# Top-32 attention and a two-layer MLP on one core: row blocks, interleaved VectorE steps, smaller MLP chunks, other weight loads

## The chip, the core and the metric

The kernel runs on one NeuronCore of a Trainium2 chip. The core has TensorE (PE in the profile, its weight loads PEld), VectorE (DVE), ScalarE (ACT), GpSimd (POOL) and SyncE (SP), which issues nearly all DMAs; each runs its own instructions in order. The metric is the device time of one execution in microseconds, median of several runs.

## The reference

For 8 batches, 8 heads, 576 positions and 64 dimensions in a head, each row of scores keeps its 32 largest values, and the rest is masked away before the softmax. The result, 4608 tokens of 512 values, goes through two matrices with a PReLU between them.

```python
scores = scale * np.matmul(q, k.transpose(0, 1, 3, 2))
kth = np.partition(scores, -top_k, axis=-1)[..., -top_k:-top_k + 1]
scores = np.where(scores >= kth, scores, -1000000000.0)
scores = scores - np.max(scores, axis=-1, keepdims=True)
attn = np.exp(scores)
attn = attn / (np.sum(attn, axis=-1, keepdims=True) + 1e-09)
attn_out = np.matmul(attn, v)
x = attn_out.transpose(0, 2, 1, 3).reshape(B * S, H * D)
h = x @ w_in                                  # 512 x 2048
g = np.maximum(h, 0.0) + alpha * np.minimum(h, 0.0)
out = g @ w_out                               # 2048 x 512
```

## The kernel before

Heads are taken in pairs (32 pairs, four for each batch). A *duo* is the work unit of the attention: 128 query rows of the two heads of a pair ("n", row block j = 0 to 3), or the last 64 rows of the four heads of two pairs ("m"). There are 18 duos in a batch and 144 in all. In batches 0 to 6 the duos go pair by pair: all four row blocks of pair e, those of pair e+1, then their "m". In the last batch they go by row block: block 0 of its four pairs, then block 1, and so on.

The main loop `for n in range(ND + 8)` is a software pipeline written out by hand. Every engine is wrapped in `Ordered`, so each runs exactly in the order of the program. One pass of the loop holds, for different duos:

- `st_phase2(n-2)` on VectorE: the largest 8 of y for both halves (`p<-y`), then eq, pk, and the threshold `KT`.
- `st_count(n-1)` on ScalarE: two sign passes `sg` with a count, biased by `p9`; `st_exit(n+1)`: the scores from PSUM to `s_sb`; `st_y(n-1)` on GpSimd: y = s times sg.
- `st_phase1(n)` on VectorE: twelve maxima over 96 values (`up` and `small`), bot, top, hi, neg, n8, and the ninth value of `p9`.
- `st_relu(n-2)` on ScalarE and `st_sub(n-2)` on GpSimd: pushes the values under the threshold down; `st_exp(n-3)`: the exponential into `w`, and a transposing DMA `wT<-w` on SP.
- `st_av(n-5)` on TensorE: attention times V into `xo` (or `xm`), where V's appended column of ones gives the sum; `st_norm(n-5)` on VectorE: `rz`, the reciprocal, and `x`.
- `st_qk(n+2)` on TensorE: the scores of a later duo into `ps_sc`.
- `prep(n, 4)`: transposes K and Q of a pair that begins within four duos on TensorE (`tps`, `tpt`); ScalarE copies K to `kT`, VectorE copies Q to `qT`. `loads(n, 7)` issues the loads of K, Q and V of a pair together, `casts(n)` turns V to bf16 on GpSimd.
- `f_unit()` and `o_unit()`: the MLP in small pieces. A unit of the first matmul is four matmuls into `ph` and a ReLU into `gT`, which alternates between VectorE and ScalarE (`relu`). A part of the second is five matmuls into `pz`; four parts make 128 tokens, and the last of them is followed by ScalarE's copy `o_sb` and the output DMA. Credits `fo` and `oo` (1.9 and 1.2 per pass) decide how many pieces are issued; towards the end the credits grow.

PReLU is split: relu(h) goes through w_out scaled by 1 - alpha (`w_out_b`), and the linear rest through one 512 x 512 matrix `w_lin_b` = w_in times alpha times w_out, which `weights()` computes in the first passes. It does so in units, two for each pass: load a piece of w_in and cast it on GpSimd; load a piece of w_out and scale it twice on ScalarE; transpose w_in by DMA; four `lin` units of 16 matmuls.

A batch's x reaches the MLP (`mlp_ready`) when all its pairs are transposed (`xT<-x`, one DMA for each pair). The MLP then takes the 576 tokens as one chunk, 32 units of 288 tokens; in the last batch it takes each row block by itself.

PSUM has eight banks: four for the scores (`ps_s`), one each for `small` (`ps_d`), for `ph` and the transposes together (`ps_h`), for `pz` (`ps_z`) and for `xo` (`ps_x`). All pools in PSUM have one buffer. In SBUF the staging pool `stg` has two buffers for each of K, Q and V, `qk_p` four, `gp` two. Behind `fast_path` stands `general_path`, which runs only where a flag says that the thresholds were not found; for these inputs it does not run.

Nearly all instructions are issued through `Ordered.call`, line 31, so that the profile's rows have that line, and the tiles' names tell them apart.

Of the kernel before, what the change touches and what calls it, by code (L numbers as in the profile page):

```python
# [17 lines left out]
NG = 6  # L18
# [17 lines left out]
def fast_path(tc, q, k, v, moe_w_in, moe_w_out, moe_alpha, out, flag):  # L36
# [17 lines left out]
    for b in range(B):  # L54
        p0 = KPB * b
        if b < B - 1:
            for e in (p0, p0 + 2):
                duos += [("n", p, j) for p in (e, e + 1) for j in range(4)]
                duos.append(("m", e, e + 1))
        else:  # L60
            duos += [("n", p, j) for j in range(4) for p in range(p0, p0 + 4)]
            duos += [("m", p0, p0 + 1), ("m", p0 + 2, p0 + 3)]
# [6 lines left out]
    with ExitStack() as ctx:  # L69
        pool = lambda name, bufs, **kw: ctx.enter_context(tc.tile_pool(name=name, bufs=bufs, **kw))  # L70
        const = pool("const", 1)
        stg = pool("stg", 2)
        io = pool("io", 4)
        qk_p = pool("qk", 4)
# [3 lines left out]
        gp = pool("gp", 2)  # L78
# [6 lines left out]

        ident_f = const.tile([128, 128], FP32, name="ident_f")
        make_identity(nc, ident_f)

        small = ps_d.tile([128, 512], FP32, name="small")
        io9 = small[:, 500:509]  # L90
        for i in range(9):
            DVE.memset(io9[:, i:i + 1], float(2 * i - 63 + S))
        KT = const.tile([128, ND, 2], FP32, name="KT")
        NV = 6
        v1s = [const.tile([128, 5, 2, 65], BF16, name=f"v1_{i}") for i in range(NV)]
        for t in v1s:
            POOL.memset(t, 1.0)
        ws = [const.tile([128, 2, 640], BF16, name=f"w_{i}") for i in range(3)]
        for t in ws:
            POOL.memset(t[:, :, S:640], 0.0)  # L100
        xs = [const.tile([128, 5, 128], BF16, name=f"x_{i}") for i in range(4)]
        for t in xs:
            POOL.memset(t[64:128, 4, :], 0.0)
        w_in_b = [const.tile([128, DFF], BF16, name=f"w_in_b{i}") for i in range(4)]
        w_out_b = [const.tile([128, DMODEL], BF16, name=f"w_out_b{i}") for i in range(NFT)]
        w_lin_b = [const.tile([128, DMODEL], BF16, name=f"w_lin_b{i}") for i in range(4)]
        alpha_sb = const.tile([128, NFT], FP32, name="alpha_sb")
        alpha1m = const.tile([128, NFT], FP32, name="alpha1m")
# [9 lines left out]
        def load_one(p, which, src):  # L118
            t = stg.tile([128, 5, 128], FP32, name=f"{which}_st", tag=f"{which}_st")
            for h in range(2):  # L120
                SP.dma_start(
                    t[:, 0:4, 64 * h:64 * h + 64],
                    src[2 * p + h, 0:512, :].rearrange("(c p) d -> p c d", p=128),
                )
                SP.dma_start(t[0:64, 4, 64 * h:64 * h + 64], src[2 * p + h, 512:S, :])
            st[which, p] = t

        def transpose_one(p, which, eng):
            t = st.pop((which, p))
            dst = qk_p.tile([128, S], FP32, name=f"{which}T", tag=f"{which}T")  # L130
            copy = ACT.copy if eng is ACT else DVE.tensor_copy
# [43 lines left out]
        def st_phase1(n):  # L175
            s = T["s", n]
            o = 240 * (n % 2)
            up = two.tile([128, 2, NG // 2, 8], FP32, name="up", tag="up")
            lo = small[:, o:o + 48].rearrange("p (i g c) -> p i g c", i=2, g=NG // 2)
            top = small[:, o + 48:o + 96].rearrange("p (i g c) -> p i g c", i=2, g=NG // 2)  # L180
            hi = small[:, o + 96:o + 112].rearrange("p (i c) -> p i c", i=2)
            n8 = small[:, o + 112:o + 128].rearrange("p (i c) -> p i c", i=2)
            for i in range(2):
                for g in range(NG):
                    DVE.max(out=(lo if g % 2 else up)[:, i, g // 2, :], in_=s[:, i, GW * g:GW * g + GW])


            bot = two.tile([128, 2, NG // 2, 8], FP32, name="bot", tag="bot")
            DVE.tensor_tensor(bot, up, lo[:, :, :, ::-1], ALU.min)
            DVE.tensor_tensor(top, up, lo[:, :, :, ::-1], ALU.max)  # L190
            neg = two.tile([128, 2, 32], FP32, name="neg", tag="neg")
            for i in range(2):
                DVE.max(out=hi[:, i, :], in_=bot[:, i, :, :])
            DVE.tensor_scalar(neg[:, :, 0:24].rearrange("p i (g c) -> p i g c", g=NG // 2), top, -1.0, None, ALU.mult)
            DVE.tensor_scalar(neg[:, :, 24:31], hi[:, :, 0:7], -1.0, None, ALU.mult)
            for i in range(2):
                DVE.max(out=n8[:, i, :], in_=neg[:, i, 0:31])
            p9 = three.tile([128, 2, 9], FP32, name="p9", tag="p9", bufs=4)
            DVE.tensor_scalar(p9[:, :, 0:1], n8[:, :, 7:8], -1.0, None, ALU.mult)
            T["p9", n] = p9  # L200
# [16 lines left out]

        def st_phase2(n):
            y, p9, cs = T.pop(("y", n)), T.pop(("p9", n)), T.pop(("cs", n))
            for i in range(2):  # L220
                DVE.max(out=p9[:, i, 1:9], in_=y[:, i, :])
            eq = small[:, 240 * (n % 2) + 128:240 * (n % 2) + 146].rearrange("p (i c) -> p i c", i=2)
            DVE.tensor_tensor(eq, io9.unsqueeze(1).to_broadcast([128, 2, 9]),
                              cs.unsqueeze(2).to_broadcast([128, 2, 9]), ALU.is_equal)
            pk = two.tile([128, 2, 9], FP32, name="pk", tag="pk")
            DVE.scalar_tensor_tensor(out=pk, in0=eq, scalar=BIG, in1=p9, op0=ALU.mult, op1=ALU.mult)
            DVE.tensor_reduce(out=KT[:, n, :].unsqueeze(2), in_=pk, op=ALU.add, axis=AX.X)

# [40 lines left out]

        xT = {}  # L270
        done = {}

        def st_norm(n):
            d = duos[n]
            xo = T.pop(("xo", n))
            m, w = (128, 2) if d[0] == "n" else (64, 4)
            rz = two.tile([128, 4], FP32, name="rz", tag="rz")
            DVE.reciprocal(rz[0:m, 0:w], xo[:, :, 64])
            if d[0] == "n":
                _, p, j = d  # L280
                DVE.tensor_tensor(xs[p % 4][:, j, :].rearrange("p (h d) -> p h d", h=2), xo[:, :, 0:64],
                                  rz[:, 0:2].unsqueeze(2).to_broadcast([128, 2, 64]), ALU.mult)
            else:
                for i in range(2):
                    DVE.tensor_tensor(xs[d[1 + i] % 4][0:64, 4, :].rearrange("p (h d) -> p h d", h=2),
                                      xo[:, 2 * i:2 * i + 2, 0:64],
                                      rz[0:64, 2 * i:2 * i + 2].unsqueeze(2).to_broadcast([64, 2, 64]),
                                      ALU.mult)

        def st_xT(n):  # L290

            d = duos[n]
            ps_ = d[1:2] if d[0] == "n" else d[1:]
            for p in ps_:
                b, kk = p // KPB, p % KPB
                j = d[2] if d[0] == "n" else 4
                if b < B - 1 and j < 4:
                    continue
                if ("xT", p) not in T:
                    T["xT", p] = xp.tile([128, 5, 128], BF16, name=f"xT{kk}", tag=f"xT{kk}")  # L300
                t = T["xT", p]
                if b < B - 1:
                    SP.dma_start_transpose(t, xs[p % 4].rearrange("p a b -> p (a b)"))
                else:
                    SP.dma_start_transpose(t[:, j:j + 1, :], xs[p % 4][:, j, :])
                done[b, j] = done.get((b, j), 0) + 1
                if done[b, j] == KPB:
                    mlp_ready(b, j)
# [5 lines left out]
        def mlp_ready(b, j):  # L314
            xt = [T["xT", KPB * b + kk] for kk in range(KPB)]
            flat = [t.rearrange("p a b -> p (a b)") for t in xt]
            if b < B - 1:
                tok0, ntok = 0, S
            else:
                tok0, ntok = 128 * j, (128 if j < 4 else 64)  # L320
# [3 lines left out]
            big = ntok == S  # L324
            cw = 288 if big else 4 * ntok

            def unit(i):
                if i == 0:

                    while oq and oq[0][0] <= me - 2:  # L330
                        oq.pop(0)[1]()
                    hold["g"] = gp.tile([128, NFT, ntok], BF16, name="gT", tag="gT" if big else "gs")
                gt = hold["g"]
                ph = ps_h.tile([128, cw], FP32, name="ph", tag="h")
                if big:
                    f, t0 = i // 2, 288 * (i % 2)
                    for kk in range(4):
# [472 lines left out]
```

## Time and profile before

| | |
|---|---|
| runs | 1291.47, 1293.12, 1298.55 us; median 1293.12 |
| profiled execution | 1296.23 us, span 1294.2 us |
| mean granted TensorE clock | 0.797 |
| busy: TensorE, VectorE, ScalarE, GpSimd | 881.2, 896.7, 836.6, 759.8 us |
| chain that ended last | DVE 46%, PE 24%, ACT 13%, DMA 6%, issue 4%, SPq 3%, POOL 3% |
| starts of `s_sb<-ps_sc` for duos 0, 18, 36, 54, 72, 90, 108, 126 | 11.3, 183.5, 335.1, 469.4, 602.6, 738.6, 875.3, 1040.2 us |

No engine is busy for more than 69% of the span. A row of the profile has the start or the busy time, then engine, operation, output and inputs. Where a row names a releaser in brackets, the engine sat idle for that long before it, until the releaser was done. "Granted clock" is the share of full speed that TensorE was given.

### The profile page before, as it was taken

How to read it: one execution, taken by the hardware profiler on the slowest of the kernel's cores; microseconds unless marked ns; L12 is line 12 of the kernel's file. 1: busy time of each engine (PE TensorE's matmuls, PEld its weight loads, DVE VectorE, ACT ScalarE, POOL GpSimd, SP SyncE). 2: the span in 40 equal slices, each digit the busy share in tenths (PEclk: the TensorE clock that was granted, in tenths of full speed). 3: DMA queues.
4: the chain of work that ended last, by engine and by line, in shares of the span. 5: the costliest groups of instructions: out<-in, count | busy, mean ns of one | idle time of the engine just before them, and what ended most of it. 6: DMA issues, size and time to landing. Idle time of an engine off the chain costs nothing.

```text
span 1294.2 us, 18779 instructions
## 1 busy us (share of the span) xinstructions
PE 881.2 (68%) x5282; PEld 481.4 (37%) x5282; DVE 896.7 (69%) x4247; ACT 836.6 (65%) x1416; POOL 759.8 (59%) x675
## 2 busy tenths in 40 slices
PE   5542436677777867777787787687776387778655
PEld 3221213334334433443344344444343143444433
DVE  4873444788878988788878886888788276762620
ACT  3756554777777777787867775777577265663530
POOL 4873433667766777676757775777577265442530
PEclk9955567576788988998888877997788668989767
DMA  4544541426252534443433533343424413221220
GB/s 107 123 118 96 111 99 38 89 44 109 53 114 62 99 72 97 83 90 80 90 74 87 89 82 77 82 96 69 105 54 99 91 31 69 51 46 45 57 53 20
DMA packets 346000, 102.00 MB, mean 79 GB/s; under 512 B 337168, under 2 KB 337184, under 8 KB 345888
## 3 DMA queue, kind: packets, MB, share of 16 engines
q1 hardware_dynamic: 345888, 100.73, 37.5%
q8 instruction: 44, 0.72, 0.2%
q14 instruction: 68, 0.56, 0.1%
HBM read 36.71 MB, written 9.44 MB: 36 GB/s over the span
## 4 chain that ended last, share of the span: by engine, by line
DVE 46%; PE 24%; ACT 13%; DMA 6%; issue 4%; SPq 3%; POOL 3%; ACTq 0%; POOLq 0%
DVE small L31 15%; DVE p L31 11%; DVE up L31 6%; PE pz L31 6%; PE ph L31 6%; PE ps_sc L31 4%; PE tps L31 4%; SPq L31 3%; ACT sg L31 3%; DVE gT L31 3%; DMA w_st<-in_moe_w_out_dram 2%; ACT r L31 2%; DVE neg L31 2%; ACT s_sb L31 2%; DVE x L31 2%
## 5 line engine op out<-in xcount | busy, mean ns | idle before, releaser
L31 POOL TENSOR_TENSOR y<-s_sb,sg 128x576 f32<-128x576 f32 x288 | 361.8, 1277 | 409.6 <-ACT sg L31 409.6
L31 POOL TENSOR_TENSOR s_sb<-s_sb,r 128x576 f32<-128x576 f32 x288 | 361.7, 1278 | 61.9 <-ACT r L31 61.9
L31 PE MATMUL ps_sc<-kT,qT 64*128 64x64 f32 (+3 forms) x1280 | 256.3, 533 | 102.4 <-ACT s_sb L31 102.3
L31 PE MATMUL ph<-xT,w_in_b 128*128 128x288 bf16 (+2 forms) x1216 | 212.7, 316 | 162.6 <-DVE gT L31 63.2
L31 ACT ACTIVATE sg<-s_sb,p 128x576 bf16<-128x576 f32 x288 | 220.4, 767 | 66.6 <-DVE p L31 65.4
L31 DVE MAX8 p<-y 128x8 f32<-128x576 f32 x288 | 204.2, 747 | 44.2 <-POOL y L31 44.2
L31 ACT ACTIVATE r<-s_sb,KT 128x576 bf16<-128x576 f32 x288 | 207.2, 768 | 33.7 <-DVE KT L31 27.5
L31 PEld LDWEIGHTS ps_sc<-kT,qT 64*128 64x128 f32 (+1 forms) x1280 | 126.1, 216 | 268.9 <-issue 148.2
L31 DVE MAX8 small<-s_sb 128x8 f32<-128x96 f32 x864 | 216.7, 251 | 0.0
L31 DVE MAX8 up<-s_sb 128x8 f32<-128x96 f32 x864 | 211.1, 244 | 3.1 <-ACT s_sb L31 3.1
L31 PEld LDWEIGHTS <-w_in_b 128*128 128x128 bf16 x1216 | 114.8, 111 | 201.8 <-issue 164.9
L31 PE MATMUL pz<-w_out_b,gT 128*128 128x512 bf16 (+1 forms) x640 | 187.0, 420 | 0.0
L31 ACT ACTIVATE w<-s_sb 128x1152 bf16<-128x1152 f32 x144 | 165.6, 1150 | 1.1 <-POOL s_sb L31 1.1
L31 ACT COPY s_sb<-ps_sc 128x1152 f32<-128x1152 f32 x144 | 158.2, 1098 | 7.0 <-PE ps_sc L31 7.0
L31 PEld LDWEIGHTS <-wT 128*128 128x128 bf16 (+3 forms) x1600 | 106.1, 108 | 119.7 <-issue 42.9
L31 PE MATMUL xo<-v,wT 128*128 128x65 bf16 (+1 forms) x1280 | 113.1, 212 | 49.0 <-DMA wT<-w 28.2
L31 DVE TENSOR_SCALAR gT<-ph 128x288 bf16<-128x288 f32 (+2 forms) x122 | 56.7, 465 | 110.9 <-PE ph L31 110.8
L31 ACT ACTIVATE gT<-ph 128x288 bf16<-128x288 f32 (+2 forms) x122 | 50.8, 416 | 120.3 <-PE ph L31 120.3
L31 DVE COPY qT<-tps 128x512 f32<-128x512 f32 x32 | 22.1, 691 | 117.2 <-PE tps L31 117.2
L31 PEld LDWEIGHTS <-gT 128*128 128x128 bf16 (+1 forms) x640 | 71.0, 111 | 79.8 <-issue 30.8
L31 PE MATMUL pz<-w_lin_b,xT 128*128 128x512 bf16 (+1 forms) x160 | 70.6, 441 | 2.8 <-ACT o_sb L31 2.7
L31 ACT COPY kT<-tps 128x512 f32<-128x512 f32 x32 | 18.7, 584 | 74.4 <-PE tps L31 74.4
(54 smaller groups left out, 733.3 us busy)
## 6 DMA issues: line engine op xcount, KB each, us to landing
k_st<-in_k_dram SPq DMA_DIRECT2D x64, 128.0 KB, 2.5
q_st<-in_q_dram SPq DMA_DIRECT2D x64, 128.0 KB, 2.5
v_st<-in_v_dram SPq DMA_DIRECT2D x64, 128.0 KB, 2.4
out_dram<-o_sb SPq DMA_DIRECT2D x32, 256.0 KB, 2.5
w_st<-in_moe_w_in_dram SPq DMA_DIRECT2D x16, 256.0 KB, 3.7
w_st<-in_moe_w_out_dram SPq DMA_DIRECT2D x16, 256.0 KB, 3.0
wT<-w SPq DMA_TRANSPOSE x144, 3.4
k_st<-in_k_dram SPq DMA_DIRECT2D x64, 16.0 KB, 2.2
```

What stands on the lines that cost most here:

```text
L31: return self.tc.keep_in_program_order(f(*a, **kw))
```

## The change

The duos of all batches now go by row block. VectorE's steps of a pass stand in one function, `dve_slot`, where steps of duos n, n-1, n-2 and n-5 alternate, with the two `f_unit()` calls between them (`norm_a` issues `rz`, `norm_b` issues `x`); `st_av` comes first in the pass. Every ReLU is on VectorE. Outside the prologue both copies of a prep are on ScalarE. The MLP takes a batch in two chunks, 256 tokens (row blocks 0 and 1) and 320 tokens (blocks 2 to 4), with one unit for each of the 16 blocks of d_ff. x is kept by row block and transposed by one DMA for a block of four pairs. w_in comes by four casting DMAs of GpSimd's queue; w_out's loads (`w_load`) are issued apart from their use (`w_use`), and GpSimd does one of the two scalings. V is loaded apart from K and Q. Three preps stand ahead of the loop. Buffers: `stg` 3, `qk` 6, `gp` 3, `io` 2, a new `wst` 5, V tiles 8.

```diff
-        if b < B - 1:
-            for e in (p0, p0 + 2):
-                duos += [("n", p, j) for p in (e, e + 1) for j in range(4)]
-                duos.append(("m", e, e + 1))
...
+        duos += [("n", p, j) for j in range(4) for p in range(p0, p0 + KPB)]
+        duos += [("m", p0, p0 + 1), ("m", p0 + 2, p0 + 3)]
...
-        stg = pool("stg", 2)
-        io = pool("io", 4)
-        qk_p = pool("qk", 4)
+        stg = pool("stg", 3)
+        io = pool("io", 2)
+        wst = pool("wst", 5)
+        qk_p = pool("qk", 6)
...
-        gp = pool("gp", 2)
+        gp = pool("gp", 3)
...
+        def dve_slot(n):
...
+                for i in range(2):
+                    for g in range(NG):
+                        DVE.max(out=(lo if g % 2 else up)[:, i, g // 2, :],
+                                in_=s[:, i, GW * g:GW * g + GW])
+                        if i == 0 and g == 1 and on(n - 2):
+                            DVE.tensor_reduce(out=KT[:, n - 2, :].unsqueeze(2), in_=T.pop(("pk", n - 2)),
+                                              op=ALU.add, axis=AX.X)
+                bot = two.tile([128, 2, NG // 2, 8], FP32, name="bot", tag="bot")
+                DVE.tensor_tensor(bot, up, lo[:, :, :, ::-1], ALU.min)
+                DVE.tensor_tensor(top, up, lo[:, :, :, ::-1], ALU.max)
...
+            if on(n - 5):
+                norm_a(n - 5)
+            if on(n):
+                neg = two.tile([128, 2, 32], FP32, name="neg", tag="neg")
+                for i in range(2):
+                    DVE.max(out=hi[:, i, :], in_=bot[:, i, :, :])
+                DVE.tensor_scalar(neg[:, :, 0:24].rearrange("p i (g c) -> p i g c", g=NG // 2), top,
+                                  -1.0, None, ALU.mult)
+            if on(n - 5):
+                norm_b(n - 5)
+            if on(n - 1):
...
+                DVE.tensor_tensor(eq, io9.unsqueeze(1).to_broadcast([128, 2, 9]),
+                                  cs.unsqueeze(2).to_broadcast([128, 2, 9]), ALU.is_equal)
+                DVE.max(out=p9[:, 0, 1:9], in_=y[:, 0, :])
+            if on(n):
+                DVE.tensor_scalar(neg[:, :, 24:31], hi[:, :, 0:7], -1.0, None, ALU.mult)
+            f_unit()
+            if on(n):
+                for i in range(2):
+                    DVE.max(out=n8[:, i, :], in_=neg[:, i, 0:31])
+            if on(n - 1):
+                DVE.max(out=p9[:, 1, 1:9], in_=y[:, 1, :])
+            if on(n):
...
+                DVE.tensor_scalar(p9n[:, :, 0:1], n8[:, :, 7:8], -1.0, None, ALU.mult)
+            f_unit()
+            if on(n - 1):
...
+                DVE.scalar_tensor_tensor(out=pk, in0=eq, scalar=BIG, in1=p9, op0=ALU.mult, op1=ALU.mult)
...
+        def chunk_of(b, j):
+            if b < B - 1:
+                return (b, 0, 2) if j < 2 else (b, 2, 5)
+            return (b, j, j + 1)
...
+            SP.dma_start_transpose(xT[c][:, :, o:o + m], xs.pop((b, j))[0:m, :])
...
-                    while oq and oq[0][0] <= me - 2:
+                    while oq and oq[0][0] <= me - 3:
...
-                    relu(gt[:, f, t0:t0 + 288], ph)
+                DVE.tensor_scalar(gt[:, e_n * i:e_n * i + e_n, :].rearrange("p a t -> p (a t)"), ph,
+                                  0.0, None, ALU.max)
...
-                ACT.activation(w_out_b[f], s, AF.Copy, scale=alpha1m[:, f:f + 1])
-                ACT.activation(hold["wl"][:, f, :], s, AF.Copy, scale=alpha_sb[:, f:f + 1])
+                ACT.activation(w_out_b[f], s, AF.Copy, scale=alpha1m[:, f:f + 1])
+                POOL.tensor_scalar(hold["wl", f // 8][:, f % 8, :], s, alpha_sb[:, f:f + 1], None, ALU.mult)
...
+                if ("v", p) not in loaded and first[p] <= n + ahead - 4:
+                    loaded.add(("v", p))
                     load_one(p, "v", vv)
...
-                    transpose_one(p, "k", ACT)
-                    transpose_one(p, "q", DVE)
+                    transpose_one(p, "k", ACT.copy)
+                    transpose_one(p, "q", DVE.tensor_copy if n < 0 else ACT.copy)
...
-                if p not in cast and p in loaded and first[p] <= n + 3:
+                if p not in cast and first[p] <= n - 2:
...
+        for kk in range(4):
+            POOL.dma_start(w_in_b[kk], moe_w_in[128 * kk:128 * kk + 128, :])
         for n in range(ND + 8):
-            loads(n, 7)
+            loads(n, 6)
...
-            end = n >= ND - 14
-            fo = min(fo + (4.5 if end else 1.9), 6.0)
-            oo = min(oo + (2.5 if end else 1.2), 4.0)
+            end = n >= ND - 12
+            fo = min(fo + (4.5 if end else 1.9), 5.0)
+            oo = min(oo + (2.6 if end else 1.25), 4.0)
+            if on(n - 5):
+                st_av(n - 5)
             if on(n - 1):
                 st_count(n - 1)
             if on(n + 1):
                 st_exit(n + 1)
             if on(n - 1):
                 st_y(n - 1)
+            dve_slot(n)
...
             casts(n)
             o_unit()
             if on(n + 2):
                 st_qk(n + 2)
             o_unit()
             if on(n - 5):
                 st_xT(n - 5)
-            prep(n, 4)
+            prep(n, 3)
+            for _ in range(2):
+                if n >= 1 and w_load:
+                    w_load.pop(0)()
+                if n >= 3 and w_use:
+                    w_use.pop(0)()
```

While `w_use` still holds units, neither `f_unit` nor `o_unit` issues anything.

## The prediction

> **What bounds the kernel now.** I read the chain that ended last (46% VectorE, 24% TensorE) and then divided the span by its loop passes. One pass of the main loop is called a slot here; it issues the steps of duos n+2 to n-5. The scores' copies `s_sb<-ps_sc` (one for each slot) start at 11.3 us (first), 216 us (duo 20), 335.1, 469.4, 602.6, 738.6, 875.3 us (every 18th from duo 36), 1040.2 (duo 126) and 1211 us (the last). So there are a stage in which the weights are made (205 us), batches of 133 to 137 us, the last batch, and 83 us behind the last copy. An undisturbed slot on VectorE, from the timeline:
> ```profile
> 701.80 1.41 DVE L31 MAX8 p<-y 128x8 f32<-128x576 f32 x2
> 703.13 0.16 DVE L31 TENSOR_TENSOR small<-small,cs 128x18 f32<-128x18 f32 x1
> 703.63 0.25 DVE L31 MAX8 up<-s_sb 128x8 f32<-128x96 f32 x1
> 705.68 0.20 DVE L31 TENSOR_TENSOR bot<-up,small 128x48 f32<-128x48 f32 x1
> 707.29 0.16 DVE L31 TENSOR_SCALAR p<-small 128x2 f32<-128x2 f32 x1
> 707.77 0.45 DVE L31 TENSOR_SCALAR gT<-ph 128x288 bf16<-128x288 f32 x1
> 708.13 1.41 DVE L31 MAX8 p<-y 128x8 f32<-128x576 f32 x2
> ```
> The columns are start and duration. No row waits for another engine, and the slot is 6.33 us: 5.97 of steps and 0.36 for one ReLU (two in three have one on VectorE). 18 of these are 113 us; the 20 us above them are four transposes of K and Q per batch ("preps") and one wait for xT. TensorE at full clock:
> ```profile
> 712.30 0.40 PE L31 MATMUL pz<-w_lin_b,xT 128*64 128x512 bf16 x1
> 713.49 1.30 PE L31 MATMUL ps_sc<-kT,qT 64*128 64x512 f32 x8
> 714.79 0.65 PE L31 MATMUL ph<-xT,w_in_b 128*128 128x288 bf16 x4
> 715.28 0.78 PE L31 MATMUL xo<-v,wT 128*128 128x65 bf16 x10
> ```
> From start to start a part of the second matmul takes 1.19, the scores 1.30, a unit of the first matmul 0.49, attention times V 0.78. At half clock they take up to twice that. The stretches show when the clock falls (column 2: TensorE's busy time in 3.41 us; then the granted clock after the other engines):
> ```profile
> 546.17:549.59 3.42, 2.25 (x15) 1.11 (x13) 2.76 (x15) 1.30 (x2) 2.17 (x2) 1.00 0.28 53
> 549.59:553.00 3.41, 1.53 (x10) 0.88 (x8) 0.77 (x2) 2.68 (x7) 1.04 (x1) 1.00 0.23 43
> 553.00:556.41 3.41, 3.21 (x19) 1.98 (x19) 3.34 (x16) 2.40 (x4) 1.96 (x3) 0.54 0.02 5
> 556.41:559.83 3.42, 2.72 (x16) 1.38 (x15) 3.15 (x17) 2.24 (x5) 2.95 (x5) 0.96 0.34 63
> ```
> 2.25 busy of 3.42 keeps full clock, 1.53 is followed by half, and a stretch 3.21 busy brings it back. Over the whole trace the limits lie near 0.55 and 0.9.
>
> **Part 1, VectorE's steps.** The dependent small steps stand 0.20 to 0.24 apart (703.13, 703.33, 703.54; 705.80, 706.04), independent ones 0.08 to 0.12. Putting other steps between shrinks some six gaps: a bare slot of 5.97 - 0.69 = 5.28. But all ReLUs now go to VectorE, two per slot at 0.36: 6.0. The q copies (0.69 + 0.22) go to ScalarE. By this part alone a slot falls from 6.33 to 6.0.
>
> **Part 2, a new loop with TensorE.** The order of instructions shows: TensorE runs av(n-5), unit A, unit B, part, scores, second part, prep; `ps_h` has one buffer, so B waits for A's ReLU, which now stands behind the first y maximum, 4.1 us into VectorE's slot. And `rz`, which waits for av, has moved forward to 2.3 us into the slot. So the loop is: rz to ReLU A 1.72 (starts as above), ReLU 0.45, handing over 0.05, B 0.49, part 1.19, scores 1.30, av 0.78, handing over 0.07 = 6.05 with one part; 7.24 with two; under 6.0 with none. Before, av had 4 us to spare, since `rz` came last. The credits give, in the 14 slots of a batch without a prep, five with one part, five with two, three with none and one without units (5.5): 30.2 + 36.2 + 18.0 + 5.5 = 89.9. Two slots with the doubled av (1.55 for 0.78) add 1.6, and the one output copy that falls behind the scores (ScalarE held 2.5, of which 1.2 are spare) adds 1.3: 92.8.
>
> **Part 3, preps.** All four of a batch now fall on consecutive slots, and ScalarE makes both copies:
> ```profile
> 479.58 0.66 PE L31 MATMUL tps<-ident_f,k_st 128*128 128x128 f32 x4 [0.88 <-ACT gT L31]
> 480.91 0.27 PE L31 MATMUL tpt<-ident_f,k_st 64*128 64x64 f32 x1 [0.68 <-ACT kT L31]
> 481.49 1.05 PE L31 MATMUL tps<-ident_f,q_st 128*128 128x128 f32 x4 [0.30 <-ACT kT L31]
> ```
> K takes 1.91 from start to start, Q about 1.85 at full clock. Queued behind the copies are ScalarE's sign passes, then GpSimd's y, then VectorE's y maximum, ReLU A, B, the scores and the next prep: sign to first y 2.3 (0.95 and 1.27), maximum and step 0.75, ReLU 0.5, B 0.49, part 1.19, scores 1.30, 3.76 = 10.3; 11.5 with two parts. Two of each: 43.6. Before, a prep cost about 4.4 above its slot; so it does now.
>
> **Part 4, the DMA queue.** V is loaded later and with three buffers: the fourth pair's V waits for the first pair's cast, two slots on, and SP is in order, so wT of two duos waits behind it. The trace has that in the last batch, whose tiles already come by row block:
> ```profile
> 1003.33 0.84 POOL L31 CAST v<-v_st 128x512 bf16<-128x512 f32 x2
> 1004.20 2.13 SPq L31 DMA_DIRECT2D v_st<-in_v_dram  x4
> 1006.42 1.38 SPq L31 DMA_TRANSPOSE wT<-w  x1
> 1009.91 1.06 PE L31 MATMUL xo<-v,wT 128*128 128x65 bf16 x10 [10.63 <-DMA wT<-w]
> ```
> After: sign(n) at 0, y to 3.75, subtract to 6.3, cast to 7.1, three loads to 8.7, wT landed (3.4) at 12.2; av wanted it at 7.9. So 4.4 us per batch (bounds 0, if GpSimd runs a slot ahead, and 10.6, the row above). K and Q of the fourth pair wait likewise for a prep, but there wT has a slot to spare: nothing. xT in one DMA per block lands (2.6) as av ends: nothing, against some 2 us before; without that cover 1 us twice per batch.
>
> **Part 5, the clock.** In a prep slot TensorE is about 45% busy from the K transposes to unit B, under the 0.55 of the stretches; half clock for one or two stretches of 3.41 then falls on B, part and scores, and loses 1.7 to 3: I take 2, so 8 per batch. After the wait of part 4, 2.5. A one-part slot has a gap of 1.7 us, 0.51 busy at worst, on the limit: 0 to 10 per batch; the drops in smooth slots of before were fewer than half, so 4. Sum 14.5 (bounds 0 and 22). The Trainium skill ("TensorE: Matmul & The Clock Gate", HAM oscillation) asks only for no gaps above about 3.4 us, and would leave the clock full in all but the V wait: 12 us less per batch, 1256 in all. The stretch with 1.53 us busy fell without such a gap, so the trace decides.
>
> Batch: 92.8 + 43.6 + 4.4 + 14.5 = 155, against 134.5.
>
> **Part 6, the weights.** Before, ScalarE waited for w_out's DMAs:
> ```profile
> ACT w_out_b L31 <- DMA w_st<-in_moe_w_out_dram: 47.7, 12, 7.4
> ```
> Now loads run two slots ahead, and GpSimd takes half the scaling. Start: three preps ahead of the loop, first full slots from 39 us. Slots 3 to 10: ScalarE 5.1 + 1.43, GpSimd 5.1 + twice 0.61 to 1.13 (its cast, and its two-input step scaled): 7.0 each, and 2 for V casts, to 97; slot 11 7; `lin` slots 8.5, 8.5, 12.7 (waits for w_inT, 4.5 from issue), then three preps with the rest, 11 each, and one 10.5. Duo 20's copy at 180 to 190, for 216. The casting DMAs have 80 us: nothing.
>
> **Part 7, the end.** Chunks of 256 and 320 leave less work for the last batch: slots 125 to 141 add up to 149 (171 before, where a drain of queued parts took 26), and 5 for clock; the last 83 us keep their order: 237 from duo 126 on.
>
> **Sum.** Slots 19 to 124 are six batches less two preps: 932 - 25 = 907. 185 + 907 + 237 = 1329 us span. The profiled run was 1296.2 with a span of 1294.2, and the median 1293.1: 1329 + 2 - 3 = 1328.
>
> **Rivals.** (A) The clock holds, as the bursts join up: batch 141, 185 + 6 x 141 - 21 + 232 = 1242, less 2 for the run: 1240. For it: part 2's work is denser. Against: the 0.55. It decides from a clock loss below 8 us per batch, where the total passes 1293. (B) TensorE's loop and the V wait are hidden too, VectorE at 6.0 is the bound: batch 127, 1157. Against: one buffer in `ps_h`. (C) The weight stage stays at 216 and the V wait is the 10.6 shown: 1328 + 31 + 37 = 1396. (D) The interleaving saves nothing since the waits on VectorE itself remain: eight slots at 6.7, 5 per batch, 1358; it is in the range.
>
> **How the numbers follow.** 0.5% is about what a measurement tells from no change. Forecast (with D) 0.52, C 0.07, A 0.24, B 0.09, between forecast and A within 0.5% 0.08. So faster 0.33, same 0.08, slower 0.59. Range: A with a start of 175 gives 1230; the forecast with a clock loss of 22 and a start of 195 gives 1380. B and most of C stay out. The forecast's own range is 1300 to 1375.
>
> **What would show it.** Batches of about 155 between every 18th `s_sb` copy; `DVE rz <- PE xo` above 100 us in the waits (30.4 before); granted clock in mid-batches at 0.7 to 0.8; ScalarE's `kT` and `qT` waiting for `tps` over 2 us each; one wait `xo <- DMA wT` of some 4 us per batch; ScalarE's wait for w_st gone. Batches under 145 prove me wrong, and `rz` without waits proves part 2 wrong.

## The result: 1345 us, 3.8% slower, and the profile after

The changed kernel takes 1345.41 us (median of 4 runs, 1337.55 to 1352.53), the kernel before 1295.84 us on the same chip: a ratio of 1.0377, 95% interval 1.0301 to 1.0454. The profiled execution took 1352.53 us with a span of 1350.8, at a mean granted clock of 0.808 (0.797 before).

The page of the changed kernel, the chain that ended last, by engine; VectorE and TensorE have changed places (46% and 24% before):
```profile
PE 46%; DVE 24%; POOL 9%; ACT 8%; issue 6%; DMA 5%; SPq 1%; ACTq 0%; POOLq 0%
```
Busy are TensorE 916.3, VectorE 858.1, ScalarE 807.1, GpSimd 771.6 us (881.2, 896.7, 836.6, 759.8 before). VectorE and ScalarE are busy for less, GpSimd for 12 us more, and TensorE for 35 us more, though it has no more matmuls (5228 rows for 5282). The span grew by 56.6 us, and most of the account is in waits. From the waits of the changed kernel (total, times, longest):
```profile
DVE rz L31 <- PE xo L31: 257.3, 82, 8.7
PE ph L31 <- DVE gT L31: 211.9, 121, 4.7
ACT kT L31 <- PE tps L31: 127.7, 29, 8.3
PE xm L31 <- DMA wT<-w: 24.9, 7, 4.8
```
The first two of these, in the kernel before:
```profile
DVE rz L31 <- PE xo L31: 30.4, 7, 7.5
PE ph L31 <- DVE gT L31: 63.2, 68, 2.8
```
VectorE waits for attention times V, TensorE for a ReLU. The last two of the changed kernel are the preps and the wait behind V's loads. ScalarE's 47.7 us of waiting for w_out is gone.

The scores' copies of duos 0, 18, 36 ... 126 start at 22.5, 178.3, 330.3, 489.2, 647.1, 804.1, 960.9 and 1114.5 us. Two of these batches, as windows of the changed kernel (after the length: busy time and instructions of PE, PEld, DVE, ACT, POOL; then clock, DMA share, GB/s):
```profile
647.10:804.10 157.00, 113.90 (x621) 58.06 (x628) 106.03 (x537) 99.43 (x166) 92.89 (x81) 0.77 0.37 72
804.10:960.90 156.80, 111.46 (x621) 56.91 (x628) 106.11 (x537) 99.54 (x168) 92.97 (x81) 0.79 0.37 72
```
The two batches of before that began at 335.1 and 469.4 us took 134.3 and 133.2 us at clocks of 0.86 and 0.88. The second:
```profile
469.40:602.60 133.20, 99.16 (x628) 54.07 (x628) 111.44 (x531) 101.39 (x175) 93.28 (x81) 0.88 0.42 86
```
VectorE is busy for 5 us less per batch (106.0 for 111.4), and the batch is 23 us longer. By stretches the span grew by 56.6 us: 5.2 less up to duo 18, the same from there to duo 36, 79 more over the five batches from duo 36 to duo 126, and 17.7 less from there to the end.

**A plain slot** shows the forecast loop. Timeline of the changed kernel, start and duration:
```profile
721.90 0.17 DVE L31 RECIPROCAL rz<-xo 128x2 f32<-128x2 f32 x1 [2.24 <-PE xo L31]
723.57 0.48 DVE L31 TENSOR_SCALAR gT<-ph 128x320 bf16<-128x320 f32 x1
724.11 0.70 PE L31 MATMUL ph<-xT,w_in_b 128*128 128x320 bf16 x4 [1.59 <-DVE gT L31]
```
From here TensorE runs a part, the scores (725.82) and attention times V (727.05) without a gap, and the next `rz` starts at 727.88: once round in 5.98 us. VectorE has no wait between these two `rz` either. So with one part in the slot, the loop and VectorE's own steps take equally long; the 2.24 us of waiting stand behind a slot with two parts.

**A slot with a prep**, between the scores' copies of 647.09 and 659.59 us:
```profile
649.03 1.01 PE L31 MATMUL ph<-xT,w_in_b 128*128 128x256 bf16 x4 [2.35 <-DVE gT L31]
650.40 1.91 PE L31 MATMUL pz<-w_out_b,gT 128*64 128x512 bf16 x4
652.24 2.14 PE L31 MATMUL ps_sc<-kT,qT 64*128 64x512 f32 x8
655.00 0.59 ACT L31 COPY kT<-tps 128x512 f32<-128x512 f32 x1 [4.42 <-PE tps L31]
658.06 0.78 ACT L31 ACTIVATE sg<-s_sb,p 128x576 bf16<-128x576 f32 x1
658.95 0.17 DVE L31 RECIPROCAL rz<-xo 128x2 f32<-128x2 f32 x1 [6.00 <-PE xo L31]
```
ScalarE, which is in order, waits 4.42 us for the transposes, since TensorE reaches them only behind unit B, a part and the scores, and these run at half clock (2.14 for the scores that take 1.30). The sign passes come after that. VectorE meanwhile waits 6.00 us.

**The slot behind V's loads**, in the same batch:
```profile
684.12 0.84 POOL L31 CAST v<-v_st 128x512 bf16<-128x512 f32 x2
684.98 1.62 SPq L31 DMA_DIRECT2D v_st<-in_v_dram  x3
690.22 2.26 PE L31 MATMUL xm<-v,wT 128*64 128x65 bf16 x20 [4.20 <-DMA wT<-w]
```
The cast ends, V's loads start, `wT` follows them, and TensorE has waited 4.20 us for it.

### The profile page after: what moved, and what is told of

It is laid out like the page before. It is cut to its first block, busy times and chain, and to the rows that moved or that the text cites. A ratio compares the mean times of both kernels' runs of the same rounds, so it can differ in the third digit from the quotient of the medians.

```text
span 1350.8 us, 18673 instructions
## 1 busy us (share of the span) xinstructions
PE 916.3 (68%) x5228; PEld 484.9 (36%) x5282; DVE 858.1 (64%) x4294; ACT 807.1 (60%) x1337; POOL 771.6 (57%) x677
## 4 chain that ended last, share of the span: by engine, by line
PE 46%; DVE 24%; POOL 9%; ACT 8%; issue 6%; DMA 5%; SPq 1%; ACTq 0%; POOLq 0%
PE pz L31 14%; PE ps_sc L31 13%; PE ph L31 9%; DVE p L31 8%; DVE small L31 6%; POOL y L31 5%; DVE gT L31 4%; PE tps L31 3%; PE xo L31 2%; DVE up L31 2%; ACT sg L31 2%; POOL s_sb L31 2%; DMA wT<-w 2%; PE xm L31 2%; DVE neg L31 2%
## 5 line engine op out<-in xcount | busy, mean ns | idle before, releaser
L31 PE MATMUL ph<-xT,w_in_b 128*128 128x256 bf16 (+3 forms) x1216 | 213.5, 321 | 252.7 <-DVE gT L31 211.9
L31 PE MATMUL ps_sc<-kT,qT 64*128 64x64 f32 (+3 forms) x1280 | 274.6, 563 | 56.4 <-ACT s_sb L31 56.4
L31 DVE MAX8 p<-y 128x8 f32<-128x576 f32 x288 | 215.8, 749 | 36.0 <-POOL y L31 36.0
L31 PEld LDWEIGHTS ps_sc<-kT,qT 64*128 64x128 f32 (+1 forms) x1280 | 135.6, 232 | 248.5 <-issue 160.7
L31 PE MATMUL pz<-w_out_b,gT 128*128 128x512 bf16 (+1 forms) x618 | 206.5, 466 | 6.9 <-issue 4.9
L31 DVE RECIPROCAL rz<-xo 128x2 f32<-128x2 f32 x128 | 21.6, 169 | 257.7 <-PE xo L31 257.3
L31 DVE TENSOR_SCALAR gT<-ph 128x256 bf16<-128x256 f32 (+2 forms) x244 | 113.6, 466 | 65.8 <-PE ph L31 63.9
L31 PEld LDWEIGHTS <-wT 128*128 128x128 bf16 (+3 forms) x1600 | 99.4, 107 | 80.2 <-DMA wT<-w 34.0
L31 ACT COPY o_sb<-pz 128x512 f32<-128x512 f32 (+1 forms) x40 | 23.2, 581 | 134.3 <-PE pz L31 134.3
L31 ACT COPY kT<-tps 128x512 f32<-128x512 f32 x32 | 18.7, 585 | 127.7 <-PE tps L31 127.7
L31 PE MATMUL pz<-w_lin_b,xT 128*128 128x512 bf16 (+1 forms) x131 | 61.8, 471 | 2.3 <-ACT o_sb L31 2.3
```

The lines of the kernel that those rows point to most:

```text
L31: return self.tc.keep_in_program_order(f(*a, **kw))
```

## Experiments

The theory is the prediction's: the loop over `rz`, dear preps, V's loads ahead of `wT`, and a clock that falls in the waits these make. Most of the experiments undo or cover one of these. Differences are between medians, to 1345.4 us of the changed kernel unless said otherwise. Ratios (with their 95% intervals) are to the kernel before, which ran beside each experiment with medians of 1295.3 to 1300.3 us, so a difference of a few us says little. Diffs are against the changed kernel unless said otherwise.

**e1: `rz` later.**
```diff
-            if on(n - 5):
-                norm_a(n - 5)
...
-            if on(n - 5):
-                norm_b(n - 5)
...
                 T["p9", n] = p9n
+            if on(n - 5):
+                norm_a(n - 5)
             f_unit()
+            if on(n - 5):
+                norm_b(n - 5)
```


> Only rz and x move: from the front of dve_slot to its end, around the second unit. Theory (a loop of TensorE and VectorE closes over rz, which waits for attention times V early in the slot): the 315 us that rz waits for xo and xm nearly vanish, slots with two parts fall from about 7.2 to 6.2 us, a batch from 157 to about 146, the whole to about 1280 us. Rival (the same loop closes right behind, over unit A's matmuls and its ReLU): rz's wait turns into waits of gT for ph, batch 152 to 157, whole 1320 to 1345 us.

1310.5 us (1.0126, 1.0076 to 1.0176): 35 less, batches of 150. In between theory and rival: the wait was for the most part handed on. Waits of e1:
```profile
DVE small L31 <- ACT sg L31: 177.9, 49, 7.4
DVE gT L31 <- PE ph L31: 104.5, 61, 7.7
DVE rz L31 <- PE xo L31: 8.8, 3, 5.6
```
`rz` hardly waits for `xo` any more (257.3 in the changed kernel). But the step eq (in `small`), which needs the count of ScalarE's sign passes, waits 177.9 us for it (8.6 in the changed kernel), and the ReLUs wait 41 us longer for their units (63.9). In the changed kernel 161.6 of the 257.3 us lie in slots with a prep. There VectorE waits for the sign passes behind K's and Q's copies when `rz` stands later, so most of what `rz` waits is the preps' price, not the loop's.

**e2: V cast two slots earlier.**
```diff
-                if p not in cast and first[p] <= n - 2:
+                if p not in cast and first[p] <= n:
```


> Only V's casts move, two slots earlier, so that the fourth pair's V load finds a free buffer. Theory (the DMA queue waits for the cast with wT behind it): TensorE's waits for wT (31 us) vanish, a batch loses 4.4 us and about 2 us of half clock, the whole falls by about 40 to about 1305 us. Rival (the wait only covers another one, of the clock or of the preps): below 10 us less, 1335 to 1345 us.

1306.6 us (1.0077, 1.0042 to 1.0112): 39 less, as the theory had it. The slot behind V's loads falls from 12.2 to 7.3 us, and TensorE's wait of `xm` for `wT` is gone from the list.

**e3: the casting DMAs later.**
```diff
-        for kk in range(4):
-            POOL.dma_start(w_in_b[kk], moe_w_in[128 * kk:128 * kk + 128, :])
...
+            if 1 <= n <= 4:
+                POOL.dma_start(w_in_b[n - 1], moe_w_in[128 * (n - 1):128 * n, :])
             dve_slot(n)
```


> Only w_in's four casting DMAs move, from ahead of the loop to its slots 1 to 4. Theory (at the start they crowd out the first loads of Q, which TensorE waits for 11.7 us): first copy of the scores at 11 to 12 us instead of 22.5, the whole about 11 us less, 1334 us. Rival (the Q load is slow for another reason, or the stage of the weights takes the gain back): first copy still at 22, or duo 20's copy still at 201, whole 1345 us.

1338.1 us (1.0340, 1.0286 to 1.0393). The median moves by 7 for the 11 of the theory, within the spread of the runs, but the rows are clear. Timelines, first of the changed kernel, then of e3:
```profile
4.78 10.11 SPq L31 DMA_DIRECT2D k_st<-in_k_dram  x3
18.09 1.08 PE L31 MATMUL tps<-ident_f,q_st 128*128 128x128 f32 x4 [11.70 <-DMA q_st<-in_q_dram]
```
```profile
4.43 1.80 SPq L31 DMA_DIRECT2D k_st<-in_k_dram  x3
6.57 1.11 PE L31 MATMUL tps<-ident_f,q_st 128*128 128x128 f32 x4 [0.30 <-ACT kT L31]
```
The first row of each is SP issuing three loads. GpSimd had issued the four casting DMAs at 2.04 us, as it waits for nothing there. The first copy of scores comes at 11.0 instead of 22.5 us, duo 20's at 187.8 instead of 201.3.

**e4: something for TensorE to do in its gaps.** Six matmuls of 256 columns after unit A, and four between the transposes of each K and each Q, written into columns of a later scores tile that nobody reads, in slots 17 to 131.
```diff
+        def keep_warm(k):
+            for _ in range(k if warm[0] >= 0 else 0):
+                PE.matmul(scores(warm[0] + 2)[:, 0, 640:896], w_in_b[0][:, 0:128], w_in_b[1][:, 0:256],
+                          start=True, stop=True)
...
                 PE.transpose(ps[:, 128 * c:128 * c + 128], t[:, c, :], ident_f)
+            keep_warm(4)
...
             f_unit()
+            keep_warm(6)
...
+            warm[0] = n if 17 <= n < ND - 12 else -1
```


> Six matmuls of 256 columns between units A and B, and four between the transposes of a prep, whose results nobody reads, fill TensorE's gaps in slots 17 to 131. Theory (gaps of 1.7 us and the preps take the clock to half): granted clock in the middle batches 0.9 or more instead of 0.78, a batch 146 to 150 instead of 157, the whole 1280 to 1310 us. Rival (the clock costs little, since a half clock falls on waits): clock up, but batch 155 or more, whole 1340 or more, since the added matmuls take up to 0.6 us of a slot themselves.

1272.1 us (0.9814, 0.9766 to 0.9862): 73 less, with 895 matmuls more. That is more than the theory had, and 1.9% faster than the kernel before. A batch of e4:
```profile
613.41:756.69 143.28, 111.98 (x761) 65.17 (x768) 105.78 (x537) 99.25 (x166) 93.01 (x81) 0.94 0.40 79
```
143.3 us at a clock of 0.94, against 157.0 at 0.77. TensorE's busy time is no larger, fillers and all.

**e5: preps apart.** They fall due 13, 8, 3 and 0 slots ahead of a batch's first duo.
```diff
+        def due(p):
+            return first[p] - 3 if p < KPB else first[p - p % KPB] + (-13, -8, -3, 0)[p % KPB]
...
-                if p not in loaded and first[p] <= n + ahead:
+                if p not in loaded and due(p) <= n + ahead - 3:
...
-                if p not in prepped and p in loaded and first[p] <= n + ahead:
+                if p not in prepped and p in loaded and due(p) <= n + ahead - 3:
```


> Only the times of the preps and of their K and Q loads: 13, 8 and 3 slots ahead of the batch and in its first slot, instead of on four consecutive slots. Theory (each prep costs some 4.4 us above its slot and 2 us of clock, wherever it stands): batch 152 to 160, whole 1325 to 1350 us, as much as after. Rival (consecutive preps lengthen one another, since ScalarE never catches up): each prep costs 3 us less, batch about 145, whole about 1270 us.

1319.3 us (1.0171, 1.0098 to 1.0245): 26 less, between theory and rival. Four consecutive preps do cost more than four apart; what e8 and e9 say of it stands below them.

**e6: Q's copy back on VectorE.**
```diff
-                    transpose_one(p, "q", DVE.tensor_copy if n < 0 else ACT.copy)
+                    transpose_one(p, "q", DVE.tensor_copy)
```


> Only the copy of Q goes back to VectorE in all preps. Theory (what closes a prep slot is the way from its last copy over the next y maximum; with Q on VectorE that engine can't do its twelve maxima meanwhile): a prep slot about 1 us longer, batch 160, whole 1350 to 1375 us. Rival (ScalarE's chain is the bound and gets 1.9 us shorter): batch 150, whole about 1300 us.

1365.8 us (1.0529, 1.0453 to 1.0605): 20 more, within the theory's range, with batches of 157 to 161. This part of the change was a gain.

**e7 and e8: together.** e7 is e1, e2 and e3 in one; e8 adds e5 and e4.

> The late rz, the early V casts and the late casting DMAs together (1310.5, 1306.6 and 1338.1 us alone). Theory (three separate terms): gains of 35, 39 and 7 add up, about 1264 us, batches about 143. Rival (two of them are the same wait seen twice): 1285 us or more.

> As the three together, with the spread preps and the filling matmuls. Theory (the clock is a separate term of some 10 us per batch): 1190 to 1215 us, faster than before. Rival (without the loop over rz the gaps no longer lie on the path, and the fillers bring little): 1240 us or more.

e7: 1260.3 us (0.9699, 0.9620 to 0.9779). The three differences (35, 39, 7) add up to 1264, as separate costs would. e8: 1189.9 us (0.9180, 0.9113 to 0.9247), batches of 133 to 136. That is the low end of the theory's 1190 to 1215.

**e9 and e10: what the clock's share is.** e9 is e1 with e4's fillers; e10 is e4 with the fillers only in the slots with a prep and the one behind them, five in a batch.
```diff
+            near = any(0 <= first[p] - 3 - n + k <= 0 for p in range(NPAIR) for k in (0, 1))
+            warm[0] = n if near and 17 <= n < ND - 12 else -1
```


> The late rz and the filling matmuls together (1310.5 and 1272.1 us alone). Theory (the loop's own price at full clock is some 7 us per batch, two-part slots at 7.2 instead of 6): 1225 to 1240 us. Rival (the late rz gained only by keeping the clock up, so that nothing is left of it with the fillers): 1260 to 1275 us.

> The filling matmuls in the five slots around the preps of each batch alone. By the steps of the prediction (8 of the 12 us of clock per batch, V's wait left out, lie in the preps): two thirds of the 73 us that all fillers gained, whole 1295 to 1305 us. Rival (the gaps of 1.7 us in the other slots cost more): 1320 us or more.

e9: 1255.4 us (0.9662, 0.9615 to 0.9710), 17 under e4, between theory and rival; batches of 140.0 for 143.3. So half of e1's 35 us is gone once the fillers hold the clock, and the place of `rz` is then worth 3 us per batch. That this half was clock is not shown: e1's mean clock is 0.814, the changed kernel's 0.808. e10: 1295.6 us (0.9991, 0.9963 to 1.0020), as forecast: 50 of the 73 us lie in these five slots.

The two also bear on e5. From e9's 140.0 us per batch, e8 differs by the earlier cast, the preps apart and the start (which lies outside a batch). The slot behind V's loads goes from 12.9 to 5.8 us, 7.1 less, and the batch to 133.3, 6.7 less. That leaves nothing for the spacing: with the fillers, preps apart are worth nothing. What e5 gained without them would then be clock, but this is not shown: e5's mean granted clock is 0.806, the changed kernel's 0.808.

**e11: the same fillers in the kernel before**, at the beginning of each pass and between the transposes; the diff is against the kernel before.
```diff
...
                 PE.transpose(ps[:, 128 * c:128 * c + 128], t[:, c, :], ident_f)
+            keep_warm(4)
...
         for n in range(ND + 8):
+            warm[0] = n + 1 if 22 <= n < ND - 14 else -1
+            keep_warm(6)
             loads(n, 7)
...
+            warm[0] = n + 2 if 22 <= n < ND - 14 else -1
             prep(n, 4)
```


> The kernel before with the same fillers: six at the head of a slot, four between the transposes of a prep, in slots 22 to 129. Theory (before, TensorE's matmuls had some 4 us to spare in a slot and lay on the path only around the preps): granted clock up from 0.87 to 0.95, a batch 4 to 8 us shorter, whole 1255 to 1275 us. Rival (half clock cost before as much as after): 1235 us or less. Second rival (nothing of it was on the path): 1290 us or more.

1286.1 us (0.9899, 0.9862 to 0.9936): 14 less than the 1300.3 us of the kernel before beside it, between the theory and its second rival. Its mean clock rose from 0.797 to 0.87, and in mid-batches from 0.85 to 0.88 to about 0.95; four batches that took 133 to 137 us take 133.4 to 133.9. The same fillers brought the changed kernel five times as much (73 us). Its clock had more to regain in mid-batches (0.77 to 0.81, to 0.92 to 0.94 in e4), but not five times as much.

**e12: the prep at the front.** e8 with one line moved.
```diff
+            prep(n, 3)
             if 1 <= n <= 4:
                 POOL.dma_start(w_in_b[n - 1], moe_w_in[128 * (n - 1):128 * n, :])
             dve_slot(n)
...
-            prep(n, 3)
```


> As e8 with only the place of the preps changed: at the front of the slot, ahead of unit A, rather than at its end. Theory (a prep costs so much because TensorE reaches its transposes only behind unit B, part and scores, and ScalarE's sign passes wait behind them): a slot with a prep takes 8.5 to 9 us instead of 11 to 13, a steady batch 122 to 126 us instead of 133 to 135, the whole 1130 to 1150 us. Rival (the wait only moves to unit A's ReLU, which waits for ps_h behind the same transposes): 1180 us or more.

1144.1 us (0.8822, 0.8796 to 0.8849), as the theory had it: faster than both kernels. From e12, a wait and the chain by engine:
```profile
ACT kT L31 <- PE tps L31: 28.2, 12, 8.1
```
```profile
DVE 41%; PE 30%; ACT 14%; POOL 7%; issue 5%; DMA 3%; SPq 0%; DVEq 0%; ACTq 0%; POOLq 0%
```
ScalarE's wait for transposes falls from 101.6 us in e8 to 28.2, slots with a prep from 10.8 to 13.1 us to 8.0 to 10.4, steady batches to 125. VectorE leads the chain again.

The order by row blocks alone, in the kernel before, was not tried; nor were the ReLUs' move to VectorE and the smaller chunks undone.

## Why the prediction was right, point by point

**The sum.** 1328 was forecast, 1345 came. In the profiled execution the three stretches are 201.3 + 913.2 + 236.3 us; the forecast was 185 + 907 + 237. The start is the term that was mis-sized. The profiled execution is the slowest of its four runs, and its start is on the long side: in e1, e2, e4, e6, e9 and e10, which begin with the same DMAs, duo 20's copy starts at 192 to 198 us.

**Batch: 155, measured 157.0 and 156.8.** The terms can be told apart by e4, where the clock hardly falls:

| term | forecast | measured |
|---|---|---|
| preps, no clock loss | 43.6 | 45.7 (e4: 12.8 + 11.2 + 11.6 + 10.1) |
| other 14 slots and V's wait | 92.8 + 4.4 = 97.2 | 97.6 (e4: 143.3 - 45.7) |
| clock | 14.5 | 13.7 (157.0 - 143.3) |

All three rows take e4's fillers as free and its clock of 0.94 as full, so they are right to a few us only. Of the single steps:

- Part 1: the plain slot above takes VectorE 5.98 us with two ReLUs and no wait, 6.0 forecast. A slot of before took 5.97 without a ReLU, so the interleaving did save.
- Part 2: once round the loop in 5.98 us, 6.05 forecast. Part 2 did not see that a second loop stands close behind it, over `ph` and the ReLU: moving `rz` frees 3 us per batch with the fillers (e9), not more.
- Part 3: the four prep slots take 12.8 + 13.4 + 12.5 + 12.9 = 51.6 us, the forecast's 43.6 with its 8 of clock. What was queued behind the copies was named rightly. That a prep costs now what it cost before, on consecutive slots too, holds with the fillers, and failed by the 26 us of e5 without them. The 4.4 us above its slot are not a property of a prep but of its place (e12).
- Part 4: 4.20 us in the row for 4.4 (12.2 less 7.9, as the part has it, are 4.3). With the clock lost behind it e2 gained 39 us, 6.5 for each of six batches; the forecast had 4.4 + 2.5.
- Part 5 is the step that decided the sign, and the rival "the clock holds" (1240) stood against it. Its 8 us for the preps are 48 in six batches, and e10 gained 50. The 4 us for the other slots were a guess between bounds of 0 and 10. That a low busy share is enough for the clock to fall stood the test, also in the plain slots, which the prediction put "at 0.51 busy at worst, on the limit". The stretch of 1.53 us in the prediction could not show this alone, since it held nothing but transposes of K and Q; the ones here hold none. Three stretches of the changed kernel that follow each other, without a prep, as windows, and then a row of the timeline:
```profile
739.31:742.72 3.41, 1.82 (x22) 1.21 (x19) 3.27 (x18) 3.04 (x4) 2.50 (x3) 1.00 0.00 0
742.72:746.13 3.41, 3.41 (x16) 1.63 (x14) 3.29 (x18) 2.17 (x6) 2.94 (x4) 0.50 0.50 96
746.13:749.54 3.41, 1.82 (x17) 1.06 (x14) 3.07 (x15) 3.41 (x4) 2.52 (x3) 1.00 0.00 0
```
```profile
742.54 1.08 PE L31 MATMUL ph<-xT,w_in_b 128*128 128x320 bf16 x4 [1.59 <-DVE gT L31]
```
  1.82 us busy of 3.41 (0.53), and the next stretch runs at half clock; that one is busy throughout, and the clock comes back. The longest gap is the 1.59 us that unit B waits for unit A's ReLU. In 66 of the 79 falls of the clock in this trace, no gap above 3.4 us reaches into the stretch before. The limit of 0.55 is rough: 20 falls follow a stretch that was busier, up to 0.68, and 14 stretches at or under 0.55 kept the clock. The Trainium skill ("TensorE: Matmul & The Clock Gate", HAM oscillation) has the rule that there be no idle gaps above some 3.4 us; by these rows and e4's 73 us, keeping to it is not enough in this kernel.
- Part 6: 185 forecast, 201.3 measured; the step that failed is "The casting DMAs have 80 us: nothing." They had 80 us for themselves, but the first loads of Q and K did not have the DMA engines: 11.5 us at the first copy (e3). With them later, duo 20's copy is at 187.8, in the forecast's 180 to 190.
- Part 7: 237 forecast, 236.3 measured.

**The other rivals.** VectorE as the bound (1157, batch 127) needs the loop, V's wait and the clock all out of the way: e12, which also has the preps apart and at the front, comes to batches of 125. The weight stage did not stay at 216 (C), and V's wait is not 10.6. The interleaving did save (against D; part 1 above).

**What would show it.** The batches, the wait of `rz`, the clock of 0.77 to 0.81 and w_out's vanished wait came as listed. Only, the wait of `rz` says less for part 2 than the prediction took it to, since 161.6 of its 257.3 us lie in slots with a prep (e1). `kT` waits 4.4 us each time (127.7 / 29), but `qT` only 0.8 (23.0 / 29): once K's transposes are reached, Q's follow.

## What to carry to other kernels

A step that makes a busy engine's instruction wait for TensorE can put TensorE's clock on the path: e4 and e11 add the same fillers, and one gains five times what the other does. That TensorE had slack before and little after fits the chain (24% and 46% TensorE) and the waits of `rz` (30.4 and 257.3 us), but no run shows it by itself. Ask too, when a long wait shows, what the engine would wait for next: most of what `rz` waited for turned up at another step in e1. Ask of each moved step which loop it closes and in which order the engines reach it; one line that moved a transpose ahead of other matmuls was worth 46 us (e8 to e12). Loads that nobody needs soon are not free at the start if they share the DMA engines with the first tiles: here they delayed the first copy of scores by 11.5 us.

## What the runs showed of the hardware

- Matmuls whose result nobody reads made the kernel 73 us faster (e4), with a mean clock of 0.908 for 0.808. The mean clock by itself says little: e7 is 85 us faster than the changed kernel at 0.773.
- TensorE fell to half clock behind a stretch of 3.41 us that was 53% busy with no gap above 1.59 us, and came back after one that was busy throughout.
- Four casting DMAs of 512 KB, issued by GpSimd at 2.04 us, stretched SP's issuing of three small loads from 1.80 to 10.11 us.
